# Attention into a squared-ReLU feed-forward layer: two buffers for the incoming words of w_in, loads further ahead, dependent steps put into later slots

## The chip, the cores and the metric

The kernel runs on one NeuronCore of one Trainium2 chip. The metric is device time in microseconds (us), the median of three runs: 1564.41 us before the change (1563.24 to 1564.85). The core has a matrix engine (PE, with its weight loads shown as PEld), a vector engine (DVE), a scalar engine (ACT), a general engine (POOL), and a sync engine (SP) that here only issues DMA transfers. Each engine takes its own instructions strictly in the order in which the program lists them, and an instruction that waits holds up all that stand behind it on that engine.

## The reference

Eight batches of twelve heads, 448 positions, head size 64. Queries and keys are RMS-normalised, softmax attention is taken, and the result goes through a two-layer feed-forward block.

```python
q_n, k_n = rmsnorm(q, g_q), rmsnorm(k, g_k)          # x / sqrt(mean(x*x) + 1e-6) * g
scores = matmul(q_n, k_n.T) / sqrt(64)
scores = scores - max(scores, -1)
attn = exp(scores); attn = attn / (sum(attn, -1) + 1e-9)
x = matmul(attn, v)                                   # -> 3584 tokens x 768
h = x @ w_in                                          # 768 x 2048, float64 weights
g = s * relu(h)**2 + b
out = g @ w_out                                       # 2048 x 768, float64 weights
```

The two weight matrices arrive as float64. The kernel reads them as pairs of 32-bit words and makes two float32 matrices of each with integer operations, a high part and a low part.

## The kernel before

**Attention.** Two heads are a pair; 6 pairs make a batch, 48 pairs in all. A pair takes 8 **slots** (W = 8), one per 128 keys of one head, so a batch is 48 slots and the attention part is 384. `for s_ in range(FIRST, NSLOT + START + 1)` writes out one slot after the other, from -22. In slot s stand: the transposed scores of chunk s (`score_t`, L396 and L399, PE), their exponential (`exponent`, L411 in the first batch, L415 later, ACT), the split of the exponential of chunk s-1 into a high and a low part (`split_e` L423 on ACT, `split_e_lo` L436 on DVE), the plain scores ten slots ahead (`score`, L358, PE) and their row maximum (`maximum`, L369, DVE), and the weighted sum over chunk s-2 (`weigh`, L455, PE). The first batch (slots 0 to 47) uses unsplit exponentials and a layout of its own (`load_rows`, `norm_rows`, `turn`, `split_turned`, L219 to L254).

**Jobs.** Everything else is put into slots by a table: `at(slot, function, arguments)`. For a pair p that starts at slot s0 = 8p these are loading rows for the norm (`load`), the norm (`norm`: square on ACT L297, sum on DVE L302, power on POOL L304 and L305), its way through DRAM (`keep`, `spread`), loading keys and queries (`load_kq`), scaling them (`scale`, POOL L321, DVE L322), splitting them (`split_kq`, ACT L340 and L341, POOL L342 and L343), and so on. A function that contains `yield` goes on in the next slot: what follows the yield stands ahead of that slot's own jobs. The whole attention part is under a manual schedule, so this written order is the order on every engine, SP's included.

**Feed-forward, first layer.** From slot 61 on, PE gets six matmuls of x @ w_in per slot (`filler`, `ffn_in`, L177) for the batch that is finished. The 16 column blocks of a batch take three slots each, so in the first round the four quarters of w_in are first read in slots 61, 73, 85 and 97. `split_x` (ACT L504, DVE L505) prepares x in slots 59, 60 and 61 of every 48.

**Converting w_in.** w_in comes in 24 pieces of 128 x 512 (6 per quarter). One piece is a 512 KB load (L121, SP), four passes on DVE (L124, L127, L129, L132), two on ACT (L125, L135) and one on POOL (L136). The raw words stand in `w64`, which has **one** buffer: a load has to wait until L129 of the piece before it is done. The generator `convert` takes a piece through three calls: L124 to L129; the next load, and L132; then L135 and L136. The list PACE says in which slots calls are made, with four calls from each entry, so that a piece takes 3.75 slots where entries are 5 apart and 2.25 slots where they are 3 apart. These calls come last in a slot but for `weigh`, behind the row maximum.

**Second layer.** After slot 397 the attention pool is given back, w_out is converted and g @ w_out is done (L683). Nothing in that part changes but the form of one argument.

The numbers at the lines in this document are those of the kernel before; in the changed kernel the same lines stand 1 to 17 further down (L124 is L125 there, L302 is L309, L505 is L514).

## Time and profile before

| | us |
|---|---|
| median of 3 runs | 1564.41 (1563.24 to 1564.85) |
| the profiled execution | 1564.78 |
| its span, first to last instruction | 1563.0 |
| start of slot 0 (first L411 on ACT) | 30.58 |
| start of slot 60 | 183.81 |
| start of slot 93 | 291.17 |
| PE busy over the whole span | 1466.8 |

The profile is one execution seen by the hardware profiler. The rows below show, for groups of instructions, the engine, the source line, the tiles out<-in, the count, busy time and mean duration in nanoseconds, and the idle time just ahead of them with what ended it. A stretch of time is always in us from the start of the span. Slots are found in it by the exponentials, since there is one per slot.

### The profile page before, as it was taken

Reading aid. Unit: us, or ns where it says so; the run is one execution under the profiler, and the core shown is the slowest. Engines: PE = TensorE matmul, PEld = TensorE weight load, DVE = VectorE, ACT = ScalarE, POOL = GpSimd, SP = SyncE. Lnnn points to the kernel's source line nnn. Section 1 sums busy time; section 2 is a strip of 40 time slices with the busy share of each in tenths; the row PEclk is TensorE's granted clock in tenths of the full one; section 3 lists DMA queues with packets and bytes.
Section 4 is the critical chain, followed back from the end, with each engine's and each line's share of the span. In section 5 each row is a group of like instructions: output and inputs, shape, how many; then the busy total and the mean of one; then the engine's idle time right before and its main releaser. Section 6 shows DMA issues by size and latency. Waiting matters only on the chain. (4 is left out here: it accounts for less than half of the span.)

```text
span 1563.0 us, 21722 instructions
## 1 busy us (share of the span) xinstructions
PE 1466.8 (94%) x7380; PEld 1347.0 (86%) x7380; DVE 904.3 (58%) x1399; ACT 816.0 (52%) x1522; POOL 735.6 (47%) x611
## 2 busy tenths in 40 slices
PE   8775679999999999999999999997999999999998
PEld 7543468889989989989989989996899999999998
DVE  6986986776676776676676675269732222222210
ACT  4654646676676676766666666435442222222210
POOL 7586757667766767767767765215600000000000
PEclk9997789999999999999999999999999999999999
DMA  4465555666666666666666653276452322322300
GB/s 112 124 170 162 170 169 175 190 185 186 191 184 187 191 180 191 192 183 188 192 181 190 191 174 115 66 239 188 132 148 75 102 85 75 107 79 79 106 21 31
DMA packets 218751, 230.86 MB, mean 148 GB/s; under 512 B 72912, under 2 KB 193744, under 8 KB 218640
## 3 DMA queue, kind: packets, MB, share of 16 engines
q1 hardware_dynamic: 218640, 229.47, 49.4%
q8 instruction: 58, 0.95, 0.3%
q14 instruction: 53, 0.43, 0.1%
HBM read 177.21 MB, written 40.84 MB: 140 GB/s over the span
## 5 line engine op out<-in xcount | busy, mean ns | idle before, releaser
L177 PE MATMUL ph<-x,wih 128*128 128x448 f32 x1536 | 491.9, 367 | 0.0
L177 PEld LDWEIGHTS ph<-x,wih 128*128 128x128 f32 x1536 | 291.7, 190 | 23.5 <-issue 0.2
L415 ACT ACTIVATE st<-st 128x448 f32<-128x448 f32 x336 | 176.6, 526 | 239.4 <-PE st L399 236.3
L369 DVE TENSOR_REDUCE nmx<-sh 112x1 fp32r<-112x448 f32 x384 | 235.7, 618 | 112.4 <-PE sh L358 110.9
L177 PE MATMUL ph<-x,wil 128*128 128x448 f32 x768 | 284.6, 371 | 0.0
L683 PE MATMUL po<-woh,gh 128*128 128x384 f32 x896 | 230.1, 336 | 9.0 <-ACT gh L670 6.5
L683 PE MATMUL po<-wol,gh 128*128 128x384 f32 x896 | 229.9, 336 | 3.4 <-POOL wol L136 3.4
L683 PE MATMUL po<-woh,gl 128*128 128x384 f32 x896 | 228.9, 335 | 0.0
L455 PE MATMUL av<-ah,vs 128*128 128x448 f32 x672 | 195.9, 373 | 22.6 <-DVE ah L436 17.8
L436 DVE TENSOR_TENSOR al<-st,ah 128x448 fp32r<-128x448 f32 x252 | 154.3, 612 | 51.4 <-ACT ah L423 42.0
L358 PE MATMUL sh<-ka,qa 128*112 128x448 f32 x384 | 149.2, 391 | 34.4 <-DVE ka L253 13.2
L423 ACT CAST ah<-st 128x448 fp32r<-128x448 f32 x336 | 179.5, 534 | 2.5
L683 PEld LDWEIGHTS po<-woh,gh 128*128 128x128 f32 x896 | 162.7, 189 | 10.6 <-ACT gh L670 7.1
L683 PEld LDWEIGHTS po<-wol,gh 128*128 128x128 f32 x896 | 162.8, 189 | 4.5 <-POOL wol L136 4.5
L396 PE MATMUL st<-qa,ka 128*128 128x448 f32 (+1 forms) x384 | 160.6, 418 | 5.5 <-DVE nmx L369 4.5
L683 PEld LDWEIGHTS po<-woh,gl 128*128 128x128 f32 x896 | 162.7, 189 | 0.6 <-DVE gl L671 0.5
L455 PEld LDWEIGHTS av<-ah,vs 128*128 128x128 f32 x672 | 127.6, 192 | 38.7 <-ACT x L504 11.4
L177 PEld LDWEIGHTS ph<-x,wil 128*128 128x128 f32 x768 | 145.7, 190 | 12.0
L358 PEld LDWEIGHTS sh<-ka,qa 128*112 128x112 f32 x384 | 107.5, 281 | 46.9 <-POOL ka L342 19.0
L496 POOL TENSOR_TENSOR u<-uz,zb 64x448 f32<-64x448 f32 x96 | 118.2, 1231 | 59.7 <-DMA zb<-z_d 55.9
L342 POOL TENSOR_TENSOR ka<-kq,ka 64x448 fp32r<-64x448 f32 x84 | 98.8, 1176 | 98.2 <-ACT ka L340 85.6
L399 PE MATMUL st<-qb,kb 128*128 128x448 f32 (+1 forms) x384 | 144.0, 375 | 0.0
(76 smaller groups left out, 2042.8 us busy)
## 6 DMA issues: line engine op xcount, KB each, us to landing
kq<-in_dram SPq DMA_DIRECT2D x84, 448.0 KB, 4.0
rb<-i_d SPq DMA_DIRECT2D x84, 448.0 KB, 5.1
r_d<-r SPq DMA_DIRECT2D x128, 224.0 KB, 3.2
r<-r_d SPq DMA_DIRECT2D x24, 1024.0 KB, 6.0
raw<-in_dram SPq DMA_DIRECT2D x42, 448.0 KB, 5.5
w64i<-in_dram SPq DMA_DIRECT2D x24, 512.0 KB, 4.5
w64o<-in_dram SPq DMA_DIRECT2D x48, 256.0 KB, 3.1
kb<-ka SPq DMA_DIRECT2D x96, 112.0 KB, 2.2
```

The costliest lines, as they stand in the source:

```text
L177: T.matmul(ph[:, :SEQ], w[:, cc, f0 : f0 + P], xs[b, cc][:, part, :], start=n == 0, stop=n == 3 * NCC - 1,)
L342: G.tensor_tensor(ka[n][D:, a], t[D:, 0], ka[n][D:, a].bitcast(F32), ALU.subtract)
L358: T.matmul(sh[:QC, :SEQ], qa[p % 2][:, a].rearrange("k (p c) -> k c p", c=NQ)[:, c], ka[p % 2][:, a], start=True, stop=True,)
L369: V.tensor_reduce(out=nmxs[p][:, c : c + 1], in_=sh[:QC, :SEQ], op=ALU.max, axis=AX.X, negate=True)
L396: T.matmul(st[:rows, :SEQ], ka[n][:, keys], qa[n][:, q], start=True, stop=False)
L399: T.matmul(st[:rows, :SEQ], kb[n][:, keys], qb[n][:, q], start=False, stop=True,)
L415: S.activation(st[:rows, :SEQ], st[:rows, :SEQ], AF.Exp)
L423: S.copy(ah[:rows], sts[i][0][:rows, :SEQ])
L436: V.tensor_tensor(al, st[:rows, :SEQ], ah[:rows].bitcast(F32), ALU.subtract)
L455: T.matmul(av[:, :SEQ], x, a, start=kc == 0 and m == 0, stop=kc == 3 and m == len(todo) - 1,)
L496: G.tensor_tensor(u[a], uzs.pop((p, j))[a], zb[a], ALU.mult)
L683: T.matmul(po[e][0][:, :HALF], x[:, fc, :], w[:, f, e * HALF : (e + 1) * HALF], start=fc == 0 and m == 0, stop=fc == NFC - 1 and m == 2,)
```

## The change

1. **Two buffers for the words.** `w64` gets two buffers. The first two pieces are loaded in slot -21, and piece i + 2 is loaded in the fourth slot of piece i (`load_piece`, at s_+3). To make room, the split values `vs` share their memory with the values `vf` of the first batch, and the unsplit values `vr` of later batches have one buffer instead of two. `vs` is filled with its ones and zeros when it is first used (slots 45 and 53) and not at the start.
2. **Pieces over five slots, one per entry of PACE.** From each entry s: L124, L125 and L127 in s, L129 in s+1, L132 in s+2, L135 in s+3, L136 in s+4. PACE becomes -18, -10, then every fifth slot from 1 to 56, then every third from 61 to 88. So two pieces are converted before slot 0, twelve in slots 1 to 60 and ten in slots 61 to 92. Before, four calls per entry made this 1 (and half of another), then until slot 73 the rest.
3. **One more yield** between the sum and the power in `norm` and `norm_rows`: POOL's part stands a slot later.
4. **Later batches earlier.** `load`, `norm` and `keep` stand two slots earlier, `load_kq`, `spread`, `scale` and `split_kq` one slot earlier. `split_kq` gets a yield between ACT and POOL, so POOL's part stays in its slot.

```diff
-PACE = (-17, *range(1, 61, 5), *range(59, 92, 3))
+PACE = (-18, -10, *range(1, 61, 5), *range(61, 91, 3))
...
-    def load_double(room, dst_hi, dst_lo, src):
+    def load_double(room, dst_hi, dst_lo, src, apart=False):
...
         S.copy(dst_hi, af)
+        if apart:
+            yield
         G.tensor_tensor(dst_lo, af, dst_hi.bitcast(F32), ALU.subtract)
...
             V.tensor_reduce(out=ssq, in_=sq, op=ALU.add, axis=AX.X)
+            yield
             ri = ap.tile([QC, n], F32, tag="ri", bufs=2, name=f"ri{p}_{j}")
...
-        vs = [ap.tile([P, NKC, 2, 3, D], F32R, name=f"vs{n}") for n in range(2)]
-        for t in vs:
-            G.memset(t[:, :, 0, 1].bitcast(F32), 1.0)
-            G.memset(t[:, :, 1, 1].bitcast(F32), 0.0)
+        vs = [None, None]
...
-                vr = vrs[p] = ap.tile([P, NKC, 2, D], F32, tag="vr", bufs=2, name=f"vr{p}")
+                vr = vrs[p] = ap.tile([P, NKC, 2, D], F32, tag="vr", name=f"vr{p}")
...
             V.tensor_reduce(out=ssq, in_=raw, op=ALU.add, axis=AX.X)
+            yield
             ri = invs[p] = ap.tile([P, n], F32, tag="ri", bufs=2, name=f"ri{p}")
...
             S.copy(qa[n][:, a], t[:, 1])
+            yield
             G.tensor_tensor(ka[n][D:, a], t[D:, 0], ka[n][D:, a].bitcast(F32), ALU.subtract)
...
-                w = ap.tile([P, WI, 2], I32, tag="w64", name=f"w64i{i}")
-                a = ap.tile([P, WI], I32, tag="wa", bufs=2, name=f"wai{i}")
-                yield load_double((w, a, hi), hi, lo, src)
+                w = ap.tile([P, WI, 2], I32, tag="w64", bufs=2, name=f"w64i{i}")
+
+
+                def words(i=i):
+                    return ap.tile([P, WI], I32, tag="wa", bufs=2, name=f"wai{i}")
+
+                yield load_double((w, words, hi), hi, lo, src, True)
...
+        def convert(n):
+
+
+            g = loaded[0] if n == 0 else turning[0]
+            if n == 0:
+                turning.append(loaded.pop(0))
+            for _ in range((2, 1, 1, 2, 1)[n]):
+                next(g, None)
+            if n == 4:
+                turning.pop(0)
...
-                at(s0 - 30, load, p)
-                at(s0 - 26, norm, p)
-                at(s0 - 22, keep, p)
+                at(s0 - 32, load, p)
+                at(s0 - 28, norm, p)
+                at(s0 - 24, keep, p)
...
-                    at(s1 - 18, load_kq, p, j)
-                    at(s1 - 18, spread, p, j)
-                    at(s1 - 14, scale, p, j)
-                    at(s1 - 12, split_kq, p, j)
+                    at(s1 - 19, load_kq, p, j)
+                    at(s1 - 19, spread, p, j)
+                    at(s1 - 15, scale, p, j)
+                    at(s1 - 13, split_kq, p, j)
...
-        for i, s_ in enumerate(chain((FIRST + 1,), PACE)):
-            for n in range(1 + 3 * (i > 0)):
-                at(s_ + n, next, converted, None)
+        for _ in range(2):
+            at(FIRST + 1, load_piece)
+        for s_ in PACE:
+            for n in range(5):
+                at(s_ + n, convert, n)
+            at(s_ + 3, load_piece)
```

Three places show how instructions move. The first is DVE before slot 0, where nmx is the row maximum, ssq the sum of squares, ka and qb the split keys and queries, wai a piece of w_in and w64i its raw words. Before:

```order
L230 TENSOR_REDUCE ssq_0_337<-sq_0_331 112x8
L369 TENSOR_REDUCE nmx_346<-sh_344 112x1
L369 TENSOR_REDUCE nmx_346<-sh_358 112x1
L369 TENSOR_REDUCE nmx_346<-sh_368 112x1
L253 TENSOR_TENSOR ka_190<-tk_1_0_348,ka_190 64x448
```

After:

```order
L233 TENSOR_REDUCE ssq_0_328<-sq_0_322 112x8
L378 TENSOR_REDUCE nmx_337<-sh_335 112x1
L125 TENSOR_SCALAR wai_339<-w64i_246 128x512
L128 SCALAR_TENSOR_TENSOR wai_339<-w64i_246,wai_339 128x512
L378 TENSOR_REDUCE nmx_337<-sh_353 112x1
L130 SCALAR_TENSOR_TENSOR wai_339<-w64i_246,wai_339 128x512
L378 TENSOR_REDUCE nmx_337<-sh_364 112x1
L133 SCALAR_TENSOR_TENSOR wai_339<-wih_242,wai_339 128x512
L257 TENSOR_TENSOR ka_184<-tk_1_0_343,ka_184 64x448
```

The four passes of the second piece now stand between the first row maxima; before, three of them stood ahead of all of this and the fourth behind it. The second place is DVE around slots 61 to 67, where x is the attention result, al and ah the low part of an exponential, zt the softmax sums. Before:

```order
L124 TENSOR_SCALAR wai_1638<-w64i_1637 128x512
L127 SCALAR_TENSOR_TENSOR wai_1638<-w64i_1637,wai_1638 128x512
L129 SCALAR_TENSOR_TENSOR wai_1638<-w64i_1637,wai_1638 128x512
L132 SCALAR_TENSOR_TENSOR wai_1638<-wih_1249,wai_1638 128x512
L505 TENSOR_TENSOR x_2_1717<-u_1157,x_2_1717 128x448
L505 TENSOR_TENSOR x_3_1720<-u_1310,x_3_1720 128x448
L436 TENSOR_TENSOR ah_1710<-st_1676,ah_1710 64x448
```

After:

```order
L125 TENSOR_SCALAR wai_1726<-w64i_1542 128x512
L128 SCALAR_TENSOR_TENSOR wai_1726<-w64i_1542,wai_1726 128x512
L445 TENSOR_TENSOR al_1755<-st_1692,ah_1739 128x448
L378 TENSOR_REDUCE nmx_1757<-sh_1751 112x1
L130 SCALAR_TENSOR_TENSOR wai_1726<-w64i_1542,wai_1726 128x512
L445 TENSOR_TENSOR al_1783<-st_1734,ah_1771 128x448
L378 TENSOR_REDUCE nmx_1757<-sh_1779 112x1
L133 SCALAR_TENSOR_TENSOR wai_1726<-wih_1326,wai_1726 128x512
```

The passes of a piece no longer stand in a block: an al and a row maximum come between them, and the number of the words (1542) shows that they were asked for long before the piece (1726), where the numbers before follow each other (1637, 1638). The third place is DVE in the later batches, in the last slot of `split_x` (slot 109 here, and again every 48 slots). Before:

```order
L480 TENSOR_SCALAR zt_2942<-zt_2942 128x7
L481 RECIPROCAL zt_2942<-zt_2942 128x7
L505 TENSOR_TENSOR x_4_3153<-u_2831,x_4_3153 128x448
L505 TENSOR_TENSOR x_5_3156<-u_3052,x_5_3156 128x448
L436 TENSOR_TENSOR al_3165<-st_3111,ah_3146 128x448
```

After:

```order
L309 TENSOR_REDUCE ssq_3150<-raw_3014 128x14
L489 TENSOR_SCALAR zt_2954<-zt_2954 128x7
L490 RECIPROCAL zt_2954<-zt_2954 128x7
L330 SCALAR_TENSOR_TENSOR kq_1_3037<-kq_1_3037,gqk,rb_1_3039 128x448
L514 TENSOR_TENSOR x_4_3162<-u_2840,x_4_3162 128x448
L514 TENSOR_TENSOR x_5_3165<-u_3061,x_5_3165 128x448
L445 TENSOR_TENSOR al_3174<-st_3113,ah_3147 128x448
```

The sum of squares and the scaling of the queries now stand ahead of that slot's al; before they came one and two slots behind it.

More of the change, by code (lines that the diff above doesn't have):

```diff
@@ L113, in psum @@
         return ps.tile([P, 512], F32, tag=bank, name=name), bank
[L115 to L120 removed]
+    def load_double(room, dst_hi, dst_lo, src, apart=False):
+        w, words, m = room
         nc.sync.dma_start(w.rearrange("p n t -> p (n t)"), src)
         yield
+        a = words()
         low, high = w[:, :, 0], w[:, :, 1]
@@ L284, in load_v @@
             else:
-                vr = vrs[p] = ap.tile([P, NKC, 2, D], F32, tag="vr", bufs=2, name=f"vr{p}")
+                vr = vrs[p] = ap.tile([P, NKC, 2, D], F32, tag="vr", name=f"vr{p}")
                 nc.sync.dma_start(vr, v[p])
         def split_v(p):
-            vr, to = vrs.pop(p), vs[p % 2]
+            n = p % 2
+            if vs[n] is None:
+                vs[n] = ap.tile([P, NKC, 2, 3, D], F32R, tag=f"vs{n}", name=f"vs{n}")
+                for m in range(2):
+                    G.memset(vs[n][:, :, m, 1].bitcast(F32), 1.0 - m)
+            vr, to = vrs.pop(p), vs[n]
             S.copy(to[:, :, 0, 0:3:2], vr)
@@ L508, in pieces, with load_piece @@
             for i, (hi, lo, src) in enumerate(parts_of_w_in()):
-                w = ap.tile([P, WI, 2], I32, tag="w64", name=f"w64i{i}")
-                a = ap.tile([P, WI], I32, tag="wa", bufs=2, name=f"wai{i}")
-                yield load_double((w, a, hi), hi, lo, src)
-        def convert():
-            todo = pieces()
-            new = next(todo)
-            next(new)
-            while new:
-                yield
-                g = new
-                for _ in range(3):
-                    next(g)
-                yield
-                new = next(todo, None)
-                if new:
-                    next(new)
-                next(g)
-                yield
-                for _ in range(GAP + 1):
-                    next(g, None)
-        converted = convert()
+                w = ap.tile([P, WI, 2], I32, tag="w64", bufs=2, name=f"w64i{i}")
+                def words(i=i):
+                    return ap.tile([P, WI], I32, tag="wa", bufs=2, name=f"wai{i}")
+                yield load_double((w, words, hi), hi, lo, src, True)
+        todo = pieces()
+        loaded = []
+        def load_piece():
+            g = next(todo, None)
+            if g is not None:
+                next(g)
+                loaded.append(g)
+        def convert(n):
[6 more added lines that the diff above has]
+                turning.pop(0)
+        turning = []
         fill = iter(())
@@ L612, in attention_then_relu2_ffn @@
                 for f, a in jobs[s_]:
-                    if f is next:
+                    if f is convert:
                         continue
@@ L628, in attention_then_relu2_ffn @@
                 for f, a in jobs[s_]:
-                    if f is next:
+                    if f is convert:
                         f(*a)
@@ L649, in pieces @@
                 m = op.tile([P, WO], F32, tag="wm", bufs=3, name=f"wmo{i}")
-                yield load_double((w, a, m), *part)
+                yield load_double((w, lambda a=a: a, m), *part)
         def squares(t):
```

3 lines of the change are left out of this document (1 added, 2 removed).

## The prediction

> **What bounds the kernel now.** I read the forty slices of the page first, then busy times by stretch, then the waits of the slow stretch, then its DVE groups.
>
> ```profile
> PE   8775679999999999999999999997999999999998
> DVE  6986986776676776676676675269732222222210
> PEclk9997789999999999999999999999999999999999
> ```
>
> A slice is 39 us. PE is full from the eighth slice on. Before that it has holes and, in the fourth to sixth slice, a lowered clock, while DVE stands at 8 and 9. So the kernel has two parts: about 290 us in which something else than PE sets the pace, and a rest bound by PE. The stretches cut at slots 0, 60 and 93 say it in numbers (columns: the stretch, its length, busy us of PE, PEld, DVE, ACT, POOL with counts, clock, DMA share, GB/s):
>
> ```profile
> 0.00:30.58 30.58, 24.48 (x165) 22.65 (x166) 18.40 (x28) 11.68 (x19) 21.20 (x34) 0.94 0.37 102
> 30.58:183.81 153.23, 108.27 (x371) 71.59 (x369) 130.67 (x184) 89.45 (x173) 105.71 (x91) 0.87 0.56 158
> 183.81:291.17 107.36, 91.19 (x380) 79.16 (x381) 80.97 (x120) 62.94 (x128) 70.93 (x55) 0.87 0.57 173
> 291.17:1010.00 718.83, 706.34 (x3459) 645.45 (x3458) 472.64 (x787) 489.65 (x999) 481.60 (x384) 1.00 0.59 177
> ```
>
> I call these the lead-in, stage A (slots 0 to 59), stage B (60 to 92) and the rest. In the rest PE is busy 706.34 of 718.83 us: a microsecond won or lost before slot 93 is one in the total. In stage A DVE is busy 130.67 of 153.23 us, more than any other engine, and idle 22.56. What ends that idle time, and what SP waits for:
>
> ```profile
> DVE wai L124 <- DMA w64i<-in_dram: 14.5, 6, 5.0
> SPq L121 <- DVE wai L129: 44.4, 14, 7.1
> PE sh L358 <- POOL ka L342: 10.3, 4, 5.3
> POOL ri L232 <- DVE ssq L230: 15.1, 4, 4.9
> POOL ri L304 <- DVE ssq L302: 14.1, 5, 5.4
> ```
>
> SP's row covers stages A and B, the others A alone. It is a ring: SP cannot ask for the next words before L129 has read the single buffer, and DVE, the busiest engine, then stands still until they land.
>
> **What a piece costs.** DVE's groups of stage A, then of stage B (busy us, mean ns, idle before and its cause):
>
> ```profile
> L129 DVE SCALAR_TENSOR_TENSOR wai<-w64i,wai 128x512 int32<-128x512 int32 x15 | 22.7, 1514 | 0.5
> L127 DVE SCALAR_TENSOR_TENSOR wai<-w64i,wai 128x512 int32<-128x512 int32 x15 | 14.8, 988 | 0.5
> L132 DVE SCALAR_TENSOR_TENSOR wai<-wih,wai 128x512 f32<-128x512 f32 x16 | 11.7, 731 | 0.0
> L124 DVE TENSOR_SCALAR wai<-w64i 128x512 int32<-128x512 int32 x15 | 11.6, 772 | 14.6 <-DMA w64i<-in_dram 14.5
> ```
>
> ```profile
> L127 DVE SCALAR_TENSOR_TENSOR wai<-w64i,wai 128x512 int32<-128x512 int32 x7 | 8.3, 1186 | 0.2
> L129 DVE SCALAR_TENSOR_TENSOR wai<-w64i,wai 128x512 int32<-128x512 int32 x7 | 7.3, 1046 | 0.2
> L132 DVE SCALAR_TENSOR_TENSOR wai<-wih,wai 128x512 f32<-128x512 f32 x7 | 6.4, 912 | 0.2
> L124 DVE TENSOR_SCALAR wai<-w64i 128x512 int32<-128x512 int32 x7 | 3.3, 477 | 7.6 <-DMA w64i<-in_dram 7.6
> ```
>
> A piece costs DVE 1514 + 988 + 731 + 772 = 4.0 us in stage A, and (8.3 + 7.3 + 6.4 + 3.3) / 7 = 3.6 in stage B. The counts say how the pieces are spread now: 15 in A, 7 in B, 2 in the lead-in. The change makes it 2, 12 and 10.
>
> **Stage A.** Three pieces leave: with the odd L132, 60.8 - 12 x 4.0 = 12.8 us of DVE work, so 130.67 becomes 117.9. Against that stands crowding. Alone, a pass is short:
>
> ```profile
> 18.43 0.69 DVE L129 SCALAR_TENSOR_TENSOR wai<-w64i,wai 128x512 int32<-128x512 int32 x1
> L136 POOL TENSOR_TENSOR wil<-wai,wih 128x512 fp32r<-128x512 f32 x15 | 19.6, 1304 | 5.2 <-ACT wih L135 5.1
> ```
>
> Three passes at 0.69 and one at 0.43 (477 ns is the mean of stage B, nearly free) are 2.5 us; the other 1.5 us of a piece come beside POOL, whose share is 105.71 / 153.23 = 69%. POOL loses three subtractions of 1304 ns and gains the memsets of `vs`, about 1 us, so 103 us in a stage of some 131 are 79%. In proportion the excess grows by 79/69, 12 x 1.5 x 0.14 = 2.5 us. That gives 120.4 of DVE work. The Trainium skill, "SBUF — State Buffer", section "SBUF: two separate sides", says why: DVE and GpSimd share a port pair that is locked for a whole instruction, so the loser does not slow down but stops. By that rule the excess could grow faster than the share; the rows allow it, and it is the last rival below.
>
> The wait for w64i goes: a load now stands seven slots ahead of its use in stage A and three in stage B, some 15 and 9 us, and its buffer is free two slots before the load is asked for. A load takes about
>
> ```profile
> 199.62 0.34 SPq L121 DMA_DIRECT2D w64i<-in_dram  x1
> 206.72 0.43 DVE L124 TENSOR_SCALAR wai<-w64i 128x512 int32<-128x512 int32 x1 [3.74 <-DMA w64i<-in_dram]
> ```
>
> 7 us where it is slow. SP's 44.4 us at L121 go too. Of the idle time, 22.56 - 14.5 = 8.1 us stay, 5.8% of 130.67 + 8.1. I take 8%, since waits like the 10.3 us of scores for POOL's ka, which now happen while DVE is held anyway, can come to the surface. 120.4 / 0.92 = 130.9, so stage A gives **-22.3 us**. Bounds: no idle time at all, -32.8; the old idle share of 14.7%, 120.4 / 0.853 = 141.2, -12.0. POOL's part of a norm a slot later and the later batches a slot or two sooner cost no instruction; they take away the 15.1 and 14.1 us for which POOL stood at L232 and L304, which is time of POOL, not of the bound, and I cost them at nothing, covered by DVE. If that cover went, POOL's 103 us would still fit.
>
> **Stage B.** Three pieces more: 80.97 + 3 x 3.6 = 91.8, and 10 x 1.1 us of excess times 0.15 for crowding make it 93.4. DVE's passes now come one at a time between al and row maximum, where before a late landing held al behind three passes. Idle at 6%: 99.4, so **-8.0 us**. Bounds: no idle time, -14.0; the present 107.36 with the three pieces on top, +10.8. PE's own work fits under that. The exponentials, one per slot, in a stretch of the rest:
>
> ```profile
> 291.17:998.00 706.83, 152.42 (x291) 1.00 0.59 178
> ```
>
> That is 2.43 us a slot where PE sets the pace, or 80 us for the 33 slots of B at full clock. The present 107.36 are at a mean clock of 0.87. The Trainium skill, "TensorE: Matmul & The Clock Gate", section "What's actually happening", has an idle window of about 3.4 us halve PE's clock; stages A and B at 0.87 and the rest at 1.00 fit that, and a PE that waits in small bits would gain from it. I count nothing for it.
>
> **Lead-in.** Four DVE passes of the second piece move in between row maxima. DVE is full there:
>
> ```profile
> 21.20 1.68 DVE L369 TENSOR_REDUCE nmx<-sh 112x1 fp32r<-112x448 f32 x3
> 22.91 0.62 DVE L253 TENSOR_TENSOR ka<-tk,ka 64x448 fp32r<-64x448 f32 x1
> 1.27 0.29 POOL masks.py:199 TENSOR_SCALAR_AFFINE_SELECT ident<-ident 128x128 f32<-128x128 f32 x1
> L331 POOL MEMSET qb<- 64x896 f32 x2 | 1.6, 840 | 0.1
> L274 POOL MEMSET vs<- 128x256 f32 x2 | 0.6, 311 | 0.0
> ```
>
> So 2.5 us go onto the way to slot 0. Of POOL's early memsets, one of qb (0.84 us) and not of vs (0.31) now stands ahead of ident's select, which PE's warm-up waits for: 0.5. With 0.2 for crowding, **+3.2 us** (bounds 0, if slack I don't see takes it, and 4.5, if the piece costs its 4.0). A second 512 KB load ahead of the rows of the second pair is needed only after 20 us.
>
> **Borders of batches.** In the rest PE stops at every end of a `split_x`, first and last of six:
>
> ```profile
> 331.92 0.44 PE L455 MATMUL av<-ah,vs 128*128 128x448 f32 x1 [1.58 <-DVE ah L436]
> 335.29 0.47 PE L455 MATMUL av<-al,vs 128*128 128x448 f32 x1 [0.48 <-DVE al L436]
> 918.68 0.44 PE L455 MATMUL av<-ah,vs 128*128 128x448 f32 x1 [1.39 <-DVE ah L436]
> 328.89 2.25 DVE L505 TENSOR_TENSOR x<-u,x 128x448 fp32r<-128x448 f32 x2 [1.15 <-ACT x L504]
> 337.35 1.07 DVE L302 TENSOR_REDUCE ssq<-raw 128x14 f32<-128x896 f32 x1
> 335.69 0.67 DVE L322 SCALAR_TENSOR_TENSOR kq<-kq,gqk,rb 128x448 f32<-128x448 f32 x1
> ```
>
> The third order listing puts the last two, 1.07 + 0.67 = 1.74 us, ahead of the al that PE awaits. On the other side POOL's halves of split_kq start a slot sooner and leave the two L505, which take 2.25 us together there, more alone. I take 0, between +1.74 and -2.06 per border.
>
> **The sum.** 3.2 - 22.3 - 8.0 + 0 = -27.1 us. The profiled execution took 1564.8 us, 1563.0 of it the span, 0.4 above the median of 1564.4. The forecast is 1564.4 - 27.1 = 1537.3, say **1537 us**.
>
> **Rivals.**
>
> *The gain is partly given back* at the borders and in stage B. For it: the 1.74 us above, and pieces now run on until slot 92, where PE had its full pace from slot 76 on. Against it: in ordinary slots DVE has 246 us of idle time in the rest. Price: 7 borders x 1.74 = 12 us, so 1549.
>
> *The change doesn't do what it says:* words still land late, since SP takes its transfers in order and load_piece stands behind others. For it: SP waits on row maxima as well. Against it: 9 us of lead against 7 at worst, in the shorter case. Then 14.5 + 7.6 us stay: 1559.
>
> *POOL's collisions eat it* (slower). In stages A and B each of 22 pieces now meets POOL four times singly instead of in one block. If every pass waited as L129 does now, a piece would cost 4 x 1.5 = 6.0 us: 22 x (6.0 - 3.9) = 46 us more, 1583. It turns the sign from 27.1 / 22 = 1.2 us per piece on, a mean above 5.1. Against it: the two stages of today, with 69% and 66% of POOL, show 4.0 and 3.6. The Trainium skill's lock, cited in stage A, is this mechanism in other words.
>
> *More than forecast:* DVE without idle time and the clock restored, 1564.4 - 32.8 - 14.0 + 3.2 = 1521.
>
> **How the numbers follow.** Forecast 0.61 (own range 1525 to 1548), partly given back 0.17, words still late 0.07, collisions 0.07, more than forecast 0.08. A range of 1523 to 1558 leaves out the collisions, the late words and part of the last case. About 0.2% (3.1 us) is what a measurement can tell. Faster by more: 0.61 + 0.17 + 0.08 + a part of the late words, 0.88. Within: 0.05. Slower: 0.07.
>
> **What would show it.** Right: no wait of L124 for w64i and none of L121 for the pass that frees the buffer; slot 0 at about 33.8, slot 60 at 165, slot 93 at 264 us; clock above 0.9 in stage B. Wrong: stage A still above 141 us, a piece above 5 us of DVE, PE stops of 3 us and more at the borders, or slot 0 after 36 us.

## The result, and the profile after

The changed kernel takes 1545.62 us (median of four runs, 1545.13 to 1547.12), the kernel before 1563.83 us beside it. The ratio is 0.9887, with a 95% interval of 0.987 to 0.9904: 18.2 us faster, where 27.1 were forecast. The profiled execution has a span of 1543.3 us, 19.7 us under the 1563.0 of before, and the comparisons below are between these two spans. In one experiment, e_no_yield, one execution of four took 2876.55 us; its time below is the median of the other three.

The forty slices of the page, the same three rows as before:

```profile
PE   7886799999999999999999999997899999999998
DVE  5989998766666766766666664389532222222210
PEclk8998899999999999999999999998899999999999
```

DVE now stands at 9 and 8 in the second to sixth slice, without the dips of before, and PE is full from the sixth, where it was from the seventh before. Busy times of stages A and B, cut at this kernel's own slots 0, 60 and 93, and, in the last row, from slot 96 to 383 (the columns are those of the prediction's table):

```profile
34.94:158.44 123.50, 99.75 (x371) 68.59 (x370) 110.46 (x168) 84.77 (x167) 106.41 (x92) 0.93 0.65 183
158.44:253.97 95.53, 82.05 (x381) 71.97 (x381) 94.12 (x135) 65.82 (x135) 83.38 (x57) 0.96 0.67 201
261.08:972.38 711.30, 694.11 (x3364) 631.38 (x3363) 466.47 (x774) 479.75 (x982) 470.89 (x377) 0.99 0.59 175
```

Slots 96 to 383 before:

```profile
298.28:997.90 699.62, 687.13 (x3364) 627.71 (x3363) 465.45 (x773) 481.34 (x984) 473.69 (x378) 1.00 0.60 179
```

So the account of the 19.7 us is this. The lead-in grew by 34.94 - 30.58 = 4.4 us. Stage A shrank from 153.23 to 123.50, by 29.7, and stage B from 107.36 to 95.53, by 11.8. At slot 93 the change was 37.2 us ahead. Of these, 11.7 were lost again between slots 96 and 383 (711.30 against 699.62), and 5.8 in the second layer, whose first matmul starts at 1049.22 here and at 1074.72 before: 494.08 us to the end against 488.28. Much of the gain was there, and nearly half of it was given back.

**The wait for words is gone.** No row of stages A and B names a wait of DVE for w64i any more, and of SP's 44.4 us for the pass that frees the buffer (L129 before, L130 now) one wait of 1.2 us is left. What SP waits for longest there now, and POOL at its power in the norm:

```profile
SPq L355 <- DVE nmx L378: 26.6, 13, 3.3
SPq L493 <- DVE zt L490: 20.7, 9, 4.6
SPq L265 <- POOL qb L352: 17.0, 11, 3.7
```

```profile
POOL ri L236 <- DVE ssq L233: 6.9, 3, 3.0
```

POOL's 14.1 us for the sum at the later norms (L304 before, L312 now) are gone too; 6.9 us of its 15.1 in the first batch's norms are left.

**A piece costs DVE less.** DVE's groups of stage A, then of stage B:

```profile
L128 DVE SCALAR_TENSOR_TENSOR wai<-w64i,wai 128x512 int32<-128x512 int32 x12 | 13.7, 1141 | 0.4
L125 DVE TENSOR_SCALAR wai<-w64i 128x512 int32<-128x512 int32 x12 | 9.5, 794 | 0.0
L133 DVE SCALAR_TENSOR_TENSOR wai<-wih,wai 128x512 f32<-128x512 f32 x12 | 9.5, 793 | 0.0
L130 DVE SCALAR_TENSOR_TENSOR wai<-w64i,wai 128x512 int32<-128x512 int32 x12 | 8.2, 680 | 0.0
```

```profile
L128 DVE SCALAR_TENSOR_TENSOR wai<-w64i,wai 128x512 int32<-128x512 int32 x10 | 15.6, 1557 | 0.3
L130 DVE SCALAR_TENSOR_TENSOR wai<-w64i,wai 128x512 int32<-128x512 int32 x10 | 8.2, 820 | 0.0
L133 DVE SCALAR_TENSOR_TENSOR wai<-wih,wai 128x512 f32<-128x512 f32 x10 | 6.8, 683 | 0.0
L125 DVE TENSOR_SCALAR wai<-w64i 128x512 int32<-128x512 int32 x10 | 4.1, 414 | 0.0
```

The means add up to 3.4 us a piece in A and 3.5 in B, against 4.0 and 3.6 before. The idle time ahead of the first pass was 14.6 and 7.6 us before; it is 0.0 twice.

**What was lost at the borders.** Six borders of batches, the ends of `split_x`, lie between slots 96 and 383. PE's two stops at the second of them, and the longer one at the third:

```profile
410.66 0.47 PE L464 MATMUL av<-al,vs 128*128 128x448 f32 x1 [0.96 <-DVE al L445]
417.74 0.60 PE L464 MATMUL av<-al,vs 128*128 128x448 f32 x1 [1.86 <-DVE al L445]
...
537.77 0.47 PE L464 MATMUL av<-al,vs 128*128 128x448 f32 x1 [1.88 <-DVE al L445]
```

Before, the stops were 1.58 and 0.48 us. DVE ahead of the second one:

```profile
413.41 1.08 DVE L309 TENSOR_REDUCE ssq<-raw 128x14 f32<-128x896 f32 x1
...
414.71 1.34 DVE L330 SCALAR_TENSOR_TENSOR kq<-kq,gqk,rb 128x448 f32<-128x448 f32 x1
415.98 1.17 DVE L514 TENSOR_TENSOR x<-u,x 128x448 fp32r<-128x448 f32 x2
417.07 0.61 DVE L445 TENSOR_TENSOR al<-st,ah 128x448 fp32r<-128x448 f32 x1
```

The al for which PE waits stands behind the sum of squares and the scaling, the two instructions that the order listing had put there. The scaling takes 1.34 us here, beside POOL, where its row of before had 0.67. The stops alone are 0.96 + 1.86 - 1.58 - 0.48 = 0.8 us longer per border. As much again is the clock. Stretches of 3.41 us around these two borders (after the length: PE busy first, the granted clock third from the end):

```profile
414.49:417.90 3.41, 1.55 (x8) 1.12 (x7) 3.38 (x7) 1.67 (x4) 3.24 (x3) 1.00 0.20 68
417.90:421.32 3.42, 3.42 (x10) 2.79 (x11) 2.24 (x5) 1.46 (x4) 1.47 (x2) 0.50 0.19 38
533.95:537.37 3.42, 1.94 (x10) 1.47 (x8) 3.38 (x7) 2.23 (x6) 3.25 (x4) 1.00 0.24 82
537.37:540.78 3.41, 3.01 (x15) 2.72 (x16) 3.00 (x6) 1.70 (x4) 2.27 (x2) 1.00 0.17 34
```

After the first stretch, in which PE was busy for 1.55 us of 3.41, the clock is halved for the next 3.41 us; after the third, with 1.94 of 3.42, it is not. The two stops are equally long. The one at 417.74 us lies inside one stretch, the one at 537.77 across the boundary of two. Half a clock came at three borders (418, 657 and 896 us), and at none before. The edge is not sharp, though. The stop before 776.34 us, at the fifth border, left PE with 1.57 us of work, and no half clock followed:

```profile
772.89:776.30 3.41, 1.57 (x8) 1.14 (x6) 3.38 (x8) 1.85 (x5) 3.24 (x4) 1.00 0.20 68
```

PE is idle for 711.30 - 694.11 = 17.2 us between slots 96 and 383, 4.7 more than the 12.5 of before, and three half-clock stretches cost 3 x 3.41 / 2 = 5.1: together 9.8 of the 11.7 us. The rest I have no row for.

**What was lost in the second layer** lies in its first 86 us, before and after:

```profile
1074.72:1160.72 86.00, 73.57 (x393) 70.26 (x392) 62.02 (x100) 44.84 (x75) 38.47 (x33) 0.94 0.55 160
```

```profile
1049.22:1135.22 86.00, 69.41 (x360) 66.15 (x359) 57.35 (x99) 41.90 (x74) 38.55 (x33) 0.88 0.53 155
```

PE gets 360 matmuls done instead of 393, and the granted clock is 0.88 instead of 0.94, about 5 us of full clock less (86.00 x 0.06). The program is the same there in all kernels of this document. One instruction of POOL stands out; POOL, DVE and PE after:

```profile
1093.99 4.20 POOL L139 TENSOR_TENSOR wol<-wao,woh 128x256 fp32r<-128x256 f32 x1 [2.23 <-ACT woh L136]
```

```profile
1094.50 1.08 DVE L128 SCALAR_TENSOR_TENSOR wao<-w64o,wao 128x256 int32<-128x256 int32 x3
1095.51 1.09 DVE L130 SCALAR_TENSOR_TENSOR wao<-w64o,wao 128x256 int32<-128x256 int32 x3
1096.52 1.08 DVE L133 SCALAR_TENSOR_TENSOR wao<-wmo,wao 128x256 f32<-128x256 f32 x3
```

```profile
1098.92 1.37 PE L700 MATMUL po<-wol,gh 128*128 128x384 f32 x2 [3.64 <-POOL wol L139]
```

The same place before:

```profile
1117.09 1.28 POOL L136 TENSOR_TENSOR wol<-wao,woh 128x256 fp32r<-128x256 f32 x1 [0.38 <-ACT woh L135]
...
1118.44 2.68 DVE L127 SCALAR_TENSOR_TENSOR wao<-w64o,wao 128x256 int32<-128x256 int32 x3
```

Before, POOL and DVE took turns: POOL's subtraction took 1.28 us, DVE's passes 2.68 / 3 = 0.9 each. After, DVE ran nine passes of 0.36 us one behind the other, POOL's subtraction stood for 4.20 us until they were through, and PE waited 3.64 us for it. Of the fourteen profiled kernels of this study, three have a subtraction of 4.2 us at this point, 44 to 46 us after the first matmul of the layer, and their second layers take 493.5, 494.1 and 495.5 us; the other eleven have none there and take 487.0 to 491.3. Since the program there is one and the same, the difference is not an edit of the change. It goes with which of POOL and DVE comes first; what decides that was not tried, and that this one instruction makes the whole 5.8 us is not shown.

### The profile page after: what moved, and what is told of

Same layout as the page of the kernel before. It is cut to its first block, busy times and chain, and to the rows that moved or that the text cites. A ratio compares the mean times of both kernels' runs of the same rounds, so it can differ in the third digit from the quotient of the medians.

```text
span 1543.3 us, 21847 instructions
## 1 busy us (share of the span) xinstructions
PE 1459.3 (95%) x7380; PEld 1343.6 (87%) x7380; DVE 892.6 (58%) x1399; ACT 812.5 (53%) x1522; POOL 748.6 (49%) x611
## 5 line engine op out<-in xcount | busy, mean ns | idle before, releaser
L700 PE MATMUL po<-woh,gh 128*128 128x384 f32 x896 | 230.9, 337 | 12.5 <-ACT gh L687 7.8
L351 POOL TENSOR_TENSOR ka<-kq,ka 64x448 fp32r<-64x448 f32 x84 | 100.4, 1196 | 108.4 <-ACT ka L348 97.3
L682 ACT ACTIVATE r<-r 128x2048 f32<-128x2048 f32 x28 | 53.7, 1917 | 168.2 <-DMA r<-r_d 168.2
```

The lines of the kernel that those rows point to most:

```text
L351: G.tensor_tensor(ka[n][D:, a], t[D:, 0], ka[n][D:, a].bitcast(F32), ALU.subtract)
L682: S.activation(r, r, AF.Square)
L700: T.matmul(po[e][0][:, :HALF], x[:, fc, :], w[:, f, e * HALF : (e + 1) * HALF], start=fc == 0 and m == 0, stop=fc == NFC - 1 and m == 2,)
```

## The experiments

All are the changed kernel with the edit shown, timed against the kernel before on the same chip. The kernel before took 1563.74 to 1565.59 us beside them, so rows are best compared by their ratios. Slots are read from the exponentials; "96-383" is the time between these slots, and the last column the second layer, all of the profiled execution. That is one execution, and not always near the median: in e_kq_back_lead it took 1538.72 us.

| kernel | us | ratio to before, 95% interval | slot 0 | slot 60 | slot 93 | slot 96 | 96-383 | 2nd layer |
|---|---|---|---|---|---|---|---|---|
| before | 1563.83 | 1 | 30.6 | 183.8 | 291.2 | 298.3 | 699.6 | 488.3 |
| after | 1545.62 | 0.9887 [0.987, 0.9904] | 34.9 | 158.4 | 254.0 | 261.1 | 711.3 | 494.1 |
| e_later_back | 1550.67 | 0.9919 [0.9903, 0.9935] | 34.7 | 167.4 | 273.4 | 282.5 | 700.9 | 487.0 |
| e_norm_back | 1560.25 | 0.9973 [0.9958, 0.9988] | 35.0 | 166.8 | 268.7 | 280.1 | 712.3 | 488.7 |
| e_lead | 1544.35 | 0.988 [0.9864, 0.9897] | 31.5 | 157.4 | 252.6 | 259.7 | 711.3 | 493.5 |
| e_one_buffer | 1556.74 | 0.9952 [0.9936, 0.9968] | 34.8 | 162.0 | 270.4 | 277.5 | 711.3 | 490.2 |
| e_kq_back | 1544.15 | 0.9873 [0.9858, 0.9889] | 32.2 | 158.9 | 259.9 | 269.8 | 704.6 | 489.9 |
| e_kq_back_lead | 1543.35 | 0.9871 [0.9854, 0.9887] | 32.3 | 158.1 | 259.0 | 267.3 | 702.3 | 490.5 |
| e_no_yield | 1543.29 | 0.9868 [0.9851, 0.9884] | 33.6 | 158.9 | 258.8 | 266.0 | 702.6 | 495.5 |
| e_old_pace | 1547.08 | 0.9888 [0.9873, 0.9902] | 30.9 | 163.7 | 257.6 | 264.7 | 712.9 | 490.4 |
| e_early | 1542.27 | 0.9855 [0.9841, 0.987] | 33.5 | 161.0 | 263.2 | 273.9 | 700.6 | 489.0 |
| e_early_lead | 1542.13 | 0.9852 [0.9838, 0.9867] | 32.1 | 159.9 | 262.1 | 272.9 | 700.5 | 490.0 |
| e_block | 1554.37 | 0.9935 [0.9918, 0.9952] | 34.6 | 162.5 | 263.1 | 270.2 | 711.4 | 491.3 |
| e_early15 | 1529.42 | 0.978 [0.9761, 0.9799] | 31.5 | 157.3 | 252.8 | 259.9 | 700.9 | 490.1 |

### Part 4 of the change undone: e_later_back

```diff
-                at(s0 - 32, load, p)
-                at(s0 - 28, norm, p)
-                at(s0 - 24, keep, p)
+                at(s0 - 30, load, p)
+                at(s0 - 26, norm, p)
+                at(s0 - 22, keep, p)
...
-                    at(s1 - 19, load_kq, p, j)
-                    at(s1 - 19, spread, p, j)
-                    at(s1 - 15, scale, p, j)
-                    at(s1 - 13, split_kq, p, j)
+                    at(s1 - 18, load_kq, p, j)
+                    at(s1 - 18, spread, p, j)
+                    at(s1 - 14, scale, p, j)
+                    at(s1 - 12, split_kq, p, j)
...
-            yield
```

The yield is the one in `split_kq`.

> The later batches are put back where they were (load, norm and keep two slots, load_kq, spread, scale and split_kq one slot later, split_kq without its yield); the rest stays as changed. Theory: the 11.7 us that the changed kernel lost between slot 93 and slot 383 come from this part alone, through PE's stops at the ends of split_x (0.96 and 1.88 us instead of 1.58 and 0.48) and the three windows of half clock behind them. Then the stops are 1.58 and 0.48 again, no half clock between 300 and 970 us, the stretch from slot 93 to slot 383 takes 707 us and not 718, and the time is about 1535 us. Rival: the loss has another cause (one buffer for the values, a later end of the conversion, another layout of the memory): the stretch stays at 718, the time at 1545. A third possibility: stages A and B need this part for their gain; then slot 93 comes later than 254 us by as much as the borders give.

Slots 96 to 383 take 700.9 us, near the 699.6 of before the change, and no half clock is left in them: the borders' loss is part 4's. But slot 96 comes 21.4 us later, the third possibility, and the time is 1550.67 and not 1535. POOL stands at the norm again (from slot 0 to slot 96):

```profile
POOL ri L312 <- DVE ssq L309: 34.2, 8, 8.6
```

The changed kernel has no such row in that stretch. So part 4 wins about twice in the first 96 slots what it loses at the borders.

### Load, norm and keep back, the rest early: e_norm_back

The first three lines of the diff above.

> Only load, norm and keep are put back by two slots; keys and queries stay a slot earlier. Theory: the sum of squares (1.08 us on DVE) ahead of the awaited al is what makes the second stop 1.88 us; without it that stop is about 0.8 us, the first stays 0.96, and with the stops that short no half clock follows: about 1.1 us per border and 4.6 us of half clock less, 1535 us. Rival: the scaling and the earlier split of keys and queries make the stops; then the stops stay within 0.3 us of 0.96 and 1.88 and the time within 3 us of 1545.

```profile
POOL ri L312 <- DVE ssq L309: 29.0, 7, 6.4
```

```profile
SPq L265 <- POOL qb L352: 48.8, 13, 6.0
```

```profile
438.25 0.53 PE L464 MATMUL av<-al,vs 128*128 128x448 f32 x1 [1.85 <-DVE al L445]
```

The stop of 1.85 us stays without the sum of squares in its place, so that sum is not what makes it; 712.3 us between slots 96 and 383 say the same. DVE's small addition to zt (L489) takes 1.08 us there, beside a subtraction of POOL, where it took 0.16 behind the sum in the changed kernel. And slot 96 comes 19 us later, so the forecast and the rival both fail. POOL stands 29.0 us for DVE's sums, and behind it in POOL's line is the split of keys and queries, for which SP now waits 48.8 us instead of 17.0. The two slots of lead for load, norm and keep together are worth those 19 us.

### The second piece earlier: e_lead

```diff
-PACE = (-18, -10, *range(1, 61, 5), *range(61, 91, 3))
+PACE = (-18, -15, *range(1, 61, 5), *range(61, 91, 3))
```

> The second piece of w_in is converted from slot -15 and not from slot -10, so its four DVE passes stand ahead of the first turned keys, where DVE was idle for 7.8 us, and not between the row maxima. Theory: these passes cost the lead-in 2.5 us directly and more through a PE that stood 4.0 us and fell to half clock; slot 0 comes at about 31 us and not 34.9, and the time is 3.5 to 4.5 us less, 1541.5. Rival: the lead-in's end is covered by stage A, which DVE bounds anyway: slot 0 is earlier, slot 60 is not, and the time stays within 1 us of 1545.6.

Slot 0 comes 3.4 us sooner, slot 60 only 1.0 and slot 96 1.4; the time falls by 1.3 us, and the ranges of the two kernels overlap. The rival is nearly right: stage A takes back most of an earlier start. That DVE's work does so is argued, not shown.

### One buffer, all else as in the change: e_one_buffer

```diff
-                w = ap.tile([P, WI, 2], I32, tag="w64", bufs=2, name=f"w64i{i}")
+                w = ap.tile([P, WI, 2], I32, tag="w64", name=f"w64i{i}")
...
-        for _ in range(2):
-            at(FIRST + 1, load_piece)
+        at(FIRST + 1, load_piece)
...
-            at(s_ + 3, load_piece)
+            at(s_ + 2, load_piece)
```

> The words of w_in have one buffer again, each load stands in the third slot of the piece before it (so three slots ahead of its use in stage A, one slot in stage B); places of the conversion and all else as changed. Theory: the ring of load and first pass is what the second buffer removed; with one buffer DVE waits again for the words, little in stage A (6 us of lead against landings of 5 to 7), 2 to 3 us for each of ten pieces in stage B, which goes from 95 to about 118 us: 1565 us. Rival: the gain came from moving and spreading the pieces, not from the buffer; DVE's wait for words stays under 5 us in all and the time under 1551.

```profile
DVE wai L125 <- DMA w64i<-in_dram: 13.9, 9, 2.3
```

The ring is back, if less than the 1565 us expected: stage B takes 108.4 us instead of 95.5, and slot 96 comes 16.4 us later. The end comes only 11.1 us later, as the second layer happened to take 3.9 us less. The second buffer, with the earlier loads that it allows, is thus worth about 16 us at slot 96 and 11 of the 18 at the end.

### Keys and queries back, norm early: e_kq_back, and with the earlier second piece: e_kq_back_lead

The last four lines and the yield of the first diff, load, norm and keep left two slots early.

> Only the second half of the move of later batches is undone: the loads of k and q, their spread, their scaling and split_kq are back in their old slots, and split_kq's copies and subtractions in one slot again; load, norm and keep stay two slots sooner. Theory: the earlier scaling and split_kq make the two PE stops at a border (0.96 and 1.88 us) and the half clock behind every second one, the earlier norm makes the gain of the first 100 slots. Then the stops are back near 1.55 and 0.5 us, no lowered clock is seen after 300 us, slots 96 to 383 take about 701 us instead of 711, slot 96 stays within 3 us of the change's 261.1, and the time is 1535 us (1532 to 1538). Rival: the first 100 slots need the earlier scaling too, since both came from the same wait of POOL; slot 96 then comes at 268 us or later, and the time is 1542 or more. A second rival: the stops come from the pieces or from the sum of squares; then they stay and the time is within 3 us of 1545.6.

> The same, and the second piece's passes start at slot -15 instead of -10. Theory: the earlier piece moved slot 0 by 3.4 us but only 1.3 us of it arrived at the end (1544.35 against 1545.6), so the two edits add up: 1 us below the run without it, 1534. Rival: with norms that are ready in time nothing absorbs the 3.4 us any more, and the gain is 3 us, 1532.

The rival of the first was right: slot 96 comes 8.7 us later, at 269.8, and the time is 1544.15. POOL's split of the keys is late now, and PE's scores wait for it, more than in the changed kernel (9.9 us there):

```profile
PEld sh L366 <- POOL ka L350: 18.6, 6, 5.3
```

At the borders the stop is 1.82 us, in both runs; slots 96 to 383 at a mean clock of 0.99 and 1.00:

```profile
421.54 0.68 PE L463 MATMUL av<-ah,vs 128*128 128x448 f32 x2 [1.82 <-DVE ah L444]
...
269.75:974.33 704.58, 691.90 (x3364) 632.21 (x3363) 446.78 (x773) 480.17 (x984) 476.89 (x377) 0.99 0.59 178
```

```profile
419.04 0.64 PE L463 MATMUL av<-ah,vs 128*128 128x448 f32 x2 [1.82 <-DVE ah L444]
...
267.29:969.64 702.35, 687.94 (x3364) 628.27 (x3363) 447.57 (x773) 479.85 (x984) 475.06 (x377) 1.00 0.60 179
```

In the first profile three of these stops were followed by half a clock, in the second none, though they are the same stops at the same places of the program. The second profile is the fastest of its four executions by 4.6 us. The difference of the two times, 0.8 us, is inside their ranges; that the two edits add up is neither shown nor refuted.

### No slot between the sum and the power: e_no_yield

```diff
             V.tensor_reduce(out=ssq, in_=raw, op=ALU.add, axis=AX.X)
-            yield
             ri = invs[p] = ap.tile([P, n], F32, tag="ri", bufs=2, name=f"ri{p}")
```

and the same in `norm_rows`.

> Undone is only the slot between DVE's sum of squares and POOL's rsqrt, in both kinds of norm; all else as in the change. Theory: POOL then stands at its queue's head for DVE's sum, as it did before for 29 us at the two lines, and what is queued behind it (subtractions of ah, split_kq, adds of x) is late for PE: a wait of POOL for ssq of 12 us or more between slots 0 and 92, slot 93 at 260 us or later instead of 254.0, the time 1551 or more. Rival: that POOL's standing is covered, as the prediction took it, and it is the two slots of lead alone that count; then slot 93 and the time stay within 3 us of 254.0 and 1545.6.

By its time the rival holds, 2.3 us from the changed kernel; by its slots neither does. POOL's wait for the sum before slot 93 is 8.9 us where 12 were expected, all of it in the first batch's norms (6.9 in the changed kernel); at the later norms it stands 8.5 us more, which the rows put down to DVE's zt (1.4 there). Slot 93 comes 4.9 us later (theory: 6 or more, rival: 3 at most), and 8.7 us are won between slots 96 and 383, since the second stop at a border is shorter:

```profile
421.27 0.47 PE L462 MATMUL av<-al,vs 128*128 128x448 f32 x1 [1.21 <-DVE al L443]
```

DVE's scaling of the queries ahead of it takes 0.68 us here, with no scaling of POOL beside it, against 1.34 in the changed kernel: 0.66 us, as much as the two stops differ (1.86 - 1.21). No stop of 1.21 us was followed by half a clock in this run between slots 96 and 383. The added slot helps where DVE is full and hurts where PE is, and a total near zero hid both.

### The old starts of the pieces: e_old_pace

```diff
-PACE = (-18, -10, *range(1, 61, 5), *range(61, 91, 3))
+PACE = (-17,-14,3,7,11,14,18,22,26,29,33,37,41,44,48,52,56,59,61,63,65,68,70,72)
```

`convert` also takes the number of the piece, so that pieces can overlap, and the two pieces of the lead-in start at other slots than in the change.

> The change with its two buffers and its spread passes, but pieces start at about the slots of before: 15 fall in slots 0 to 59 and 7 in 60 to 92, instead of 12 and 10. Theory (DVE sets the pace in both stretches, a piece costs it 3.4 to 3.5 us): slot 60 comes three pieces later, 10 us, at 168; slots 60 to 92 take 10 us less, but not under the 82 us that PE needs; so slot 93 is within 4 us of 254 and the time within 4 us of 1545.6: the pace itself is worth little. Rival: the first stretch only carries 12 pieces and the even pace is what the gain comes from: slot 93 at 264 or later, 1555 or more.

```profile
30.90:163.67 132.77, 104.38 (x371) 70.16 (x370) 123.47 (x180) 88.61 (x174) 113.55 (x96) 0.89 0.64 183
163.67:257.56 93.89, 82.70 (x380) 72.90 (x381) 79.51 (x123) 62.05 (x127) 70.90 (x53) 0.96 0.62 186
```

Three more pieces in stage A cost 132.77 - 123.50 = 9.3 us, about the 3 x 3.4 of the theory. Three fewer in stage B save 1.6 only, not 10: DVE's work falls from 94.12 to 79.51 us and the stage stays at 94. So stage A was bound by DVE and stage B was not, or no longer once its work was under 94 us. Slot 93, 3.6 us later, is within the theory's 4 us because slot 0 comes 4 us sooner, and the time, 1.5 us more, also because the second layer took 3.7 us less; the theory's half on stage B is wrong.

### The passes in a block: e_block

```diff
-            for _ in range((2, 1, 1, 2, 1)[n]):
+            for _ in range((3, 1, 3, 0, 0)[n]):
```

> The change with its pace and two buffers, but a piece's passes in a block as before (the and, the or of the high bits and the or of the low bits in one slot, the comparison in the next, the copy and subtraction in the one after). Theory: with the words there in time a block of three passes holds al and row maximum behind it in one slot of three or five, PE waits for al in that slot, and what POOL takes from DVE is the same: DVE's 3.4 to 3.5 us per piece stay, slot 93 comes 3 to 8 us later than 254.0 and the time is 1549 to 1554. Rival 1: the spread costs by meeting POOL four times, so the block is faster: slot 93 before 252, 1543 or less. Rival 2: the spread is worth nothing and the second buffer with the earlier norms is the whole gain: within 2.5 us of 1545.6.

```profile
PE av L464 <- DVE al L445: 26.0, 13, 4.4
```

In the changed kernel that row has 17.1 us. Slot 93 comes 9.2 us later, a little beyond the theory's 8, and the time is 8.8 us more; the 22 pieces of stages A and B cost DVE 77.9 us in all, against 75.6 with the passes spread (sums of the four groups). So what the spread wins is al in time, not cheaper passes: four meetings with POOL cost no more than one block.

### The moves kept for early pairs alone: e_early, e_early_lead, e_early15

```diff
+EARLY = 10
...
+            if p < EARLY:
+                yield
...
+                d = 2 * (p < EARLY)
+                at(s0 - 30 - d, load, p)
+                at(s0 - 26 - d, norm, p)
+                at(s0 - 22 - d, keep, p)
...
+                    d = p < EARLY
+                    at(s1 - 18 - d, load_kq, p, j)
```

The condition stands at the yields of `norm` and `split_kq`; `spread`, `scale` and `split_kq` are moved like `load_kq`. In the third kernel EARLY is 15. The second and third also have the second piece at slot -15. For the pairs from EARLY on, the added slot of part 3 is thus undone too.

> The change, with its moves of later batches kept only for the pairs that are normed in the first 93 slots (pairs 4 to 9); pairs 10 and up have load, norm, keep, k and q, and split_kq in the slots of before, and no added slot between DVE's sum and POOL's rsqrt. Theory: the moves gain in stages A and B, where DVE and POOL are full, and lose at the borders, where PE stops at other places and meets a lowered clock. Then slot 96 stays within 2 us of 261.1, slots 96 to 383 take 701 us as with the moves undone (700.9) instead of 711.3, and the time is 10 us below 1545.6: 1535 (1533 to 1538; the second layer varies by up to 6 us between runs of one program order, 488 to 494 us from its first matmul). Rival: the lowered clock at the borders hangs on the phase in which a stop falls (it came in three borders of six in one run and in none of another with the same stops), so slots 96 to 383 take 705 or more here too, 1540 or more.

> The same, and the second piece's passes start at slot -15 instead of -10. Theory: the lead-in is 3.4 us shorter and 1.3 us of it reaches slot 96 and the end, 1534. Rival: with the clock restored nothing takes it back, 1532 or less.

The borders are as forecast, 700.6 and 700.5 us with no half clock between slots 96 and 383. Slot 96 is not, 273.9 and 272.9, and the times are 1542.27 and 1542.13 and not 1535 and 1534; the earlier second piece shows nothing at the end. I had counted the pairs wrongly. A pair has 8 slots, so the pairs up to 9 are normed by slot 44, not 93, and the later ones of stages A and B still stood in the old slots:

```profile
POOL ri L315 <- DVE ssq L311: 28.6, 6, 6.8
```

> As the run before with the earlier second piece, but the moves are kept for pairs 6 to 14 instead of 6 to 9. The first cut was put too early: a pair has 8 slots, so pairs 10 to 14 are normed in slots 54 to 86, in stages A and B still. Theory (the moves gain as long as DVE and POOL are full and lose at the borders): POOL's wait at L315 for the sum, 25.7 us in that run, falls below 10; slot 96 comes at 260 us as with the moves kept everywhere (259.7) instead of 272.9; slots 96 to 383 take 700.5 as in that run; so the time is 1542.1 - 13 = 1529 to 1535, with the second layer's 488 to 494 us in it. Rival: PE sets the pace of slots 60 to 92 by then and something else, not the norms of pairs 10 to 14, made the 13 us; then slot 96 stays at 269 or later and the time within 3 us of 1542.

With the cut at pair 15 this wait, from slot 0 to slot 96, is

```profile
POOL ri L315 <- DVE ssq L311: 1.7, 1, 1.7
```

and from slot 96 to 383

```profile
259.87:960.74 700.87, 688.54 (x3364) 628.11 (x3363) 462.56 (x774) 480.39 (x982) 473.17 (x378) 1.00 0.59 178
```

In about that stretch, from 300 to 970 us, POOL waits again for the sums:

```profile
POOL ri L315 <- DVE ssq L311: 70.2, 31, 5.1
```

The stretch is within 1.3 us of the fastest of the table, so this wait shows no price there. Slot 96 comes 13.0 us sooner than in e_early_lead and the time is 12.7 us less: 1529.42 us (1528.99 to 1532.84), ratio 0.978. This kernel beats the change by 16.2 us. By the profiles, 10.4 of it are the borders, 1.2 the start and 4.0 the second layer, which was the luckier kind in this run.

## Why the prediction was right, and where it was not

The forecast, 1537, was 8.6 us too low, and its range of 1523 to 1558 held the time. A cause that it named is shown: one buffer put back brings the ring back and costs 16.4 us at slot 96 and 11.1 at the end. But part 4, to which it gave nothing, is worth more at slot 96, 21.4 us, and the number is near because errors of both signs met: the first two stages gave 11.2 us more than forecast, the lead-in 1.2 less, the borders and the second layer 17.5 less.

- **What bounds the kernel.** The slices were read one off: before the change PE is full from the seventh, and DVE stands at 6, 9 and 8 in the fourth to sixth; no term of the sum hangs on that. Right for the words, DVE in stage A, and the rule that a microsecond before slot 93 is one in the total: e_early15 against e_early_lead has 13.0 at slot 96 and 12.7 at the end. It holds only where the borders stay as they are.
- **The price of a piece** was too high. The passes cost 3.4 and 3.5 us, not 4.0 and 3.6. With the old starts they cost 3.7 in stage A (e_old_pace, 56.1 / 15), so part of it goes with fewer pieces there; what makes the rest is not shown. The crowding term of 2.5 us did not come, though POOL's share of stage A rose to 106.41 / 123.50 = 86%, more than the forecast's 79%. DVE's work in stage A is 110.46 us where 120.4 stood in the sum. The rival of POOL's collisions falls with it, and so does a growth of the excess with POOL's share. The lock that the Trainium skill describes ("SBUF — State Buffer", section "SBUF: two separate sides") does not say how often two engines meet, and in e_block a piece in a block cost no less, 77.9 us for the 22 pieces against 75.6.
- **Stage A: -22.3 forecast, -29.7 measured.** The mechanism was right and the size off, by the term above; the idle share, 1 - 110.46 / 123.50 = 10.6%, is higher than the 8% taken.
- **Stage B: -8.0 forecast, -11.8 measured.** DVE's work, 94.12 us, was the forecast's 93.4; its idle share is 1.5%, not 6%. The reading of what bounds the stage was too simple: e_old_pace takes 14.6 us of DVE's work out of it and gains 1.6.
- **POOL's waits, the step that failed.** "Time of POOL, not of the bound", cost at nothing, covered by DVE. The runs show it is not covered in stages A and B. With load, norm and keep two slots later POOL stands 29.0 us at L312 and slot 96 comes 19 us later; without the added slot 4.9 us at slot 93 are lost; with keys and queries one slot later, 8.7 us at slot 96. An engine that is not the bound, waiting at the head of its line, held the splits behind it, and with them SP: that reading follows the rows of e_norm_back, and no run parts the wait from the later loads. From slot 96 on the cover held, as the 70.2 us in e_early15 show. Of the change's 37 us at slot 96, 21.4 hang on part 4, to which the sum gave none. These prices overlap and do not add up.
- **Lead-in: +3.2 forecast, +4.4 measured.** The mark for slot 0, 33.8, was missed by 1.1. Much of the 4.4 varies from execution to execution: e_later_back, e_norm_back, e_early and e_kq_back are the same program up to slot 0 and reached it at 34.7, 35.0, 33.5 and 32.2. The last 10 us before slot 0 in the changed kernel and in e_kq_back:

```profile
25.00:35.00 10.00, 6.73 (x25) 5.38 (x26) 8.91 (x16) 3.09 (x6) 8.40 (x10) 0.52 0.42 113
```

```profile
22.00:32.24 10.24, 5.27 (x25) 4.37 (x26) 9.82 (x17) 4.11 (x7) 8.56 (x10) 0.83 0.45 122
```

  The clock was 0.52 in the one and 0.83 in the other.
- **Borders: 0 forecast, +11.7 us measured.** The order listing had shown the right two instructions, and the rival "partly given back" had priced them at 7 x 1.74 = 12 us. The choice of 0, on the ground that POOL's earlier halves would leave the two L505 alone, was the mistake: the first pair of L514 still took 2.25 us. The rival's price came out near for a reason that was not in it. The stops are only 0.8 us longer per border; the half clock that follows three of the six costs as much again. The bounds of +1.74 to -2.06 per border counted stops alone, and the loss, 11.7 / 6 = 1.95 us for each of the six borders in the stretch, lies outside them.
- **The clock, counted at nothing.** It rose from 0.87 to 0.93 in stage A and to 0.96 in stage B, above the mark of 0.9. The clock withheld falls by about 21 us, from 153.23 x 0.13 + 107.36 x 0.13 = 34 to 123.50 x 0.07 + 95.53 x 0.04 = 12; how much of that PE would have used, and so what part of the gain is the clock's, no run separates. The Trainium skill ("TensorE: Matmul & The Clock Gate", section "What's actually happening") speaks of a window of about 3.4 us that runs freely and of an idle window; the trace agrees on the window's length (3.41 us), and shows that the window need not be idle: half a clock followed one with 1.55 us of PE's work.
- **The rivals.** "Words still late" fell: no wait of DVE for w64i is left. "Partly given back" happened at the borders, on top of more than the forecast's gain; its 1549 us is nearer to the 1545.62 measured than the forecast. For stages A and B alone the 32.8 + 14.0 = 46.8 us of "More than forecast" came nearer to the measured 41.5 than the forecast's 30.3.
- **The second layer** was taken to move unchanged. It is the same program and took 5.8 us longer in the profiled execution.

## What to carry to other kernels

An engine that is not the bound can still cost time if it waits at the head of its line, because everything behind it waits too: before such a wait is costed at nothing, list what stands behind it and who needs that. The same move can be worth 21 us where one engine is full and cost 10 where another is; cut it to the stretch where it pays, and check by slot counts where that stretch ends. Stops of the matrix engine are to be counted with the clock that follows them: here two stops of equal length cost differently by where they fell in the windows.

## What was not expected of the hardware

- **Half-clock stretches start on a fixed grid within a run.** In the changed kernel all the lowered stretches start a multiple of 3.41 us apart, from the lead-in to the second layer, and last one such unit or a few. The border stops of 1.8 to 1.9 us lie at its edge: they can be followed by half a clock when one unit holds the whole stop, as at 417.74 us, and none that lay well across two was, as at 537.77. In the fourteen profiles, between slots 96 and 383, all 21 halved stretches follow a unit with at most 1.6 us of PE's work; some such units were followed by none, that before 776.30 us and, with 1.59 us, that before 419.08 us in e_kq_back_lead. In the second layer a unit with 2.13 us was followed by half a clock too (e_early, 1091.11 us), so this edge holds for the border stops alone. Border stops of 1.55 us, as in e_early15 at every border, were followed by none between these slots in any run. So the same code can differ by some microseconds from run to run: slots 96 to 383 of e_kq_back take 2.2 us more than those of e_kq_back_lead, with three halved stretches against none.
- **A subtraction of POOL can stand while DVE runs nine passes.** It stood for 4.20 us while DVE ran nine passes back to back. By the Trainium skill's rule of the lock, named above, one engine holds the port for a whole instruction. If it was the port that POOL waited for, which no row names, the waiting engine need not get it at the end of that instruction. In the other order, POOL first, the two took turns and a pass of DVE took 0.9 instead of 0.36 us.
